# A chunked recurrence and a softplus feed-forward in one kernel: where the lowest three weight bits are made, another fixed order, and the written order kept six steps longer

## The chip, the cores and the metric

The kernel runs on one core of a Trainium2 chip. The metric is the device time of one execution in microseconds (us); lower is better. The kernel before takes 326.82 us, the median of three runs (325.9 to 327.14). One further execution was profiled. It took 326.83 us, of which the profile covers a span of 325.1 us from the first to the last instruction.

Engines are named as the profile does: PE (TensorE matmul), PEld (its weight loads), ACT (ScalarE), DVE (VectorE), POOL (GpSimd) and SP (SyncE, which issues all loads and stores here).

## What is computed

Inputs are `x` (4 x 8 x 768 x 32), decays `a` (4 x 8 x 768), `B` and `C` (4 x 8 x 768 x 16), and two weight matrices, `w_in` (256 x 2048) and `w_out` (2048 x 256).

```python
# per batch and head, in chunks of 32 tokens, with a carried state (16 x 32)
cum = np.cumsum(log(a), axis=-1)
M = (C @ B.T) * exp(cum_i - cum_j) * causal
y = M @ x + (C @ state) * exp(cum)
state = exp(sum(log a)) * state + sum_j B_j x_j exp(cum_last - cum_j)
# then, on all 3072 tokens with the 8 heads side by side (256 columns)
h = y @ w_in
g = softplus(h)
out = g @ w_out
```

The two weight matrices come as 64-bit floating-point numbers (a float32 draw times a 64-bit scalar). The chip receives a `low` and a `high` 32-bit word for each weight and makes a float32 number of them before it splits that into a high and a low part.

## The kernel before, in words

**Units.** Tokens are worked in 24 units of 128 (4 batches of 6). For unit `i` the recurrence makes scores (`S`, matmuls into `sp`), weighs them with decays (`D` on POOL makes `rm`, `M` on DVE makes `m`), updates the state (`U`, matmuls into `zp`, then DVE; `T` on DVE spreads it to `tb`), scales B and C (`B`, `C`: `bp`, `cc`), sums into `yp` (`R`, `I`), and splits the result into a high and a low part (`G`, `X`: `xh`, `xl`). The split into high and low parts lets a matmul product be made as three fast ones. From unit 8 on, `Q`, `cr`, `v` and `e` do the same for pairs of units.

**Feed-forward.** The 3072 tokens are six blocks `j` of 512, the 2048 hidden columns are 16 tiles `k` of 128. `F j.k` (function `first`) is six matmuls into `hp`, `P j.k` is three stages (softplus `e` on ACT, high part `gh` on ACT, low part `gl` on DVE), and `Z j.k` (function `second`) is six matmuls that add into the two accumulators `acc0`, `acc1`. `H k` is the first half of an `F0.k`. Blocks 0 and 1 are worked in two halves of eight `k` each, so their sums are put aside (`K`, `L`, and `keep_sums`) and added at the end (`finish`, whose `finish_part` adds `acc` and the kept `half` into `o` on DVE, line 803, and stores it).

**Weights.** There are 16 weight steps, eight for `w_in` (even) and eight for `w_out` (odd). `w n` loads 512 KB into a buffer `wraw` (four buffers, which are shared with the `bc` rows of units 8 and up). `W n` is five stages of the generator `split_stages`, one for each time that its name stands in the order:

1. ACT makes `w` (the high word times a power of two) and the sign, in the upper half-words of a buffer `signs` (two buffers, used in turn);
2. ACT makes the three lowest bits out of the `low` word and writes them in the lower half-words of `signs`;
3. DVE: `w = (w << 3) | signs`;
4. ACT: the high part (`wih` or `woh`);
5. DVE: the low part (`wil` or `wol`).

**Order.** Everything up to the end of the string `ORDER` is issued in the order of its words, and each engine works its own instructions of them strictly in that order. A word that stands several times runs the next stage each time. `warm n` is `n` matmuls of 512 columns on zeros, whose result is not used. After the string come steps `s` from `AHEAD` = 28 to 99 (96 feed-forward steps and a lag of four). At step `s` the loop issues `Z` of step `s - 4`, `F` and `P` of step `s`, and what `fills[s]` holds of the later units (12 and up): `split_whole` at `max(s0 - 4, 28)`, `attend_scores` at `s0`, `prefetch` of the unit three later at `s0 + 1`, with `s0` = 30, 34, 38, ... for unit 12, 13, 14, .... Up to `PINNED` = 31 (that is for s = 28, 29, 30) these too are kept as written. From there on a scheduler in the compiler arranges DVE, ACT and POOL instructions by its own estimate; matmuls and SP's transfers stay as written.

In the profile nearly every instruction of the kept order stands under line 129, the line of the helper that records it, so groups are told apart by their tiles. Later DVE, ACT and POOL instructions stand under their own lines: 290 and 292 (`split_unit`), 803 (`finish_part`), 720, 726, 732 (`P`'s three stages).

Of the kernel before, what the change touches and what calls it, by code (L numbers as in the profile page):

```python
# [45 lines left out]
THREE = 2.0**-29 * (1 - 2.0**-17)  # L46
DOWN = 5.7e-5 - 0.5
# [9 lines left out]


ORDER = """
la warm3 warm5 warm2 warm3 w2 w1 hc0 hc1 kb loga un0 un2 logr loga w0 logr gb growth hc2 ft0 W2 warm1 ft0 gq0 un1 W2  # L60
hc3 D0 gq2 growth W2 un3 W1 S0 w6 D1 gd fr2 M0 W1 fr0 hc4 fr2 gq2 fr0 W1 W2 fr0 S1 fr0 B2 hc5 W1 B0 M0 gq0 U0 un4 W1
D2 I0 M1 S2 W0 U0 G0 ft2 B1 T1 W0 M2 C1 W0 S3 B3 W0 M1 ft2 U1 W0 D3 R1 U1 C2 M2 U2 gg3 I1 U2 G0 T2 U3 fr2 D4 W6 G1 R2
U3 M3 I2 fr2 T3 W6 S4 X0 C3 T4 W6 S5 hc6 C4 G2 M3 w4 R3 G2 un6 B4 D5 M4 G1 R4 un5 tl I3 w3 M4 hc7 U4 X1 I4 D6 w5 M5 H0
un7 U4 G3 un8 W2 S6 G3 W6 X2 gg6 W4 X3 H1 G4 B6 W6 F0.0 C5 T5 H2 M5 W4 M6 F0.1 D9 W4 H3 P0.1 zero W3 F0.2 M6 R5 F0.3
P0.0 D7 P0.0 S7 W4 P0.2 U6 W4 I5 P0.1 U6 I6 P0.0 W3 un9 H4 M7 W5 w7 T7 Z0.0 W3 G4 G5 P0.2 B7 X4 F0.4 C7 M7 H5 P0.1 W5
D11 R7 G6 w10 F0.5 G6 gg8 Q8 X6 U7 P0.3 I7 P0.2 Q9 F0.6 G7 W5 W3 G7 W3 P0.3 Z0.1 Q9 P0.4 G5 X7 W7 F0.7 X5 Q8 P0.3 W7
Z0.2 C8 Q8 w8 cr9 P0.6 F1.0 P0.4 W5 P0.4 Z0.3 B8 P1.0 W5 Q9 W7 P1.0 F1.1 Q9 P0.5 B9 un10 P1.0 P0.5 Z0.4 U7 W8 T8 P0.5
F1.2 W7 Q8 P0.6 w12 P0.7 S9 gg12 F1.3 P0.7 cr8 P0.7 W7 Z0.5 P1.3 P0.6 P1.1 W8 F1.4 P1.2 W8 w14 P1.3 C9 Z0.6 W8 W8 F1.5
M9 P1.1 W10 M9 P1.1 Z0.7 D8 Q10 W10 F1.6 K0 L0 P1.3 P1.2 S8 W12 F1.7 M8 Q10 P1.4 Z1.0 M8 cr10 W10 D10 un11 B10 F0.8
W10 W12 P1.4 P1.2 w9 Z1.1 P1.5 W10 W12 W14 v8 Q10 P1.5 Z1.2 v8 P0.8 P1.5 W12 e8 W12 Z1.3 e8 e8 W9 Q10 gg10 F0.9 P1.4  # L70
P0.8 P1.6 P0.8 Q11 Z1.4 P1.7 Q11 P1.7 F0.10 W9 P1.7 W14 W9 S10 P1.6 Z1.5 M10 cr11 Q11 P1.6 w11 F0.11 W14 w15 Q11 w13
C10 Z1.6 P0.11 P0.9 W9 S11 W14 F0.12 P0.11 W14 C11 W11 M11 Z1.7 M11 P0.9 M10 F0.13 W11 K1 P0.10 W11 un13 v10 L1 W9 e8
P0.9 W15 Z0.8 v10 W11 e8 P0.10 e10 P0.12 P0.10 F0.14 e10 e10 e10 Z0.9 P0.14 e10 P0.12 W11 F0.15 P0.11 W13 P0.12 Z0.10
P0.14 W13 F1.8 W15 W13 un12 P0.15 P0.14 W13 Z0.11 W15 P0.15 W13 P0.13 F1.9 P0.15 P1.8 P0.13 P0.13 Z0.12 P1.9 F1.10
Z0.13 P1.10 W15 P1.9 W15 F1.11 P1.10 P1.9 P1.10 P1.8 Z0.14 P1.11 P1.8 P1.11 Z0.15 E0 P1.11
"""
# [30 lines left out]
def recurrence_then_ffn(ctx: ExitStack, tc: tile.TileContext, fst, un, alr, w_in, w_out, const, outT):  # L107
# [24 lines left out]
    V, A, Pl = (InOrder(e) for e in (nc.vector, nc.scalar, nc.gpsimd))  # L132
# [22 lines left out]
    gd = dr.tile([NB, NH, S], F32, name="gd")  # L155
# [689 lines left out]
    def both_scores(i):  # L847
# [152 lines left out]
```

## Time and profile before

| | |
|---|---|
| median of three runs | 326.82 us (325.9 to 327.14) |
| the profiled execution | 326.83 us |
| its span | 325.1 us |
| PE busy | 318.3 us (98%), 1974 matmuls |
| DVE busy | 190.6 us (59%), 338 instructions |
| ACT busy | 191.1 us (59%), 349 instructions |
| POOL busy | 39.4 us (12%), 42 instructions |
| DMA | 36.53 MB, a mean of 112 GB/s |

A row of a group has the line, the engine, the operation, the tiles written and read, the shape and the count, then the busy time, the mean of one in ns, and the idle time of the engine just ahead of them with what ended it. A row of the timeline has the start, the duration, the same names, and in brackets the idle time ahead of it. A table of stretches gives, for each, the busy time of the engines with instruction counts in brackets, the clock, the DMA share and GB/s. A matmul's end is modelled, so that two matmuls 227 ns apart are shown with 390 ns each; a PE that is shown as busy may still have small gaps.

### The profile page before, as it was taken

What the parts mean: (1) busy time and instruction counts of PE and PEld (TensorE: products, weight loads), DVE (VectorE), ACT (ScalarE), POOL (GpSimd) and SP (SyncE); (2) the same over time, 40 slices, a digit from 0 to 9 for tenths busy, and PEclk for the clock granted to TensorE, in tenths of its full rate; (3) what the DMA queues carried; (4) which work ended last, traced back from release to release, by engine and by line L of the source; (5) the groups of instructions that cost most, each with busy time, mean ns of one, the idle gap of its engine ahead of it and who ended that gap; (6) DMA issues with size and microseconds to landing.
All of it is one profiled execution on the core that took longest, in us unless ns stands there. A gap on an engine that the chain in (4) does not pass through costs nothing.

```text
span 325.1 us, 5266 instructions
## 1 busy us (share of the span) xinstructions
PE 318.3 (98%) x1974; PEld 255.7 (79%) x1974; DVE 190.6 (59%) x338; ACT 191.1 (59%) x349; POOL 39.4 (12%) x42
## 2 busy tenths in 40 slices
PE   8999999999999999899999999999999999999996
PEld 3568888888878888588888888888888888888885
DVE  3799767889584566775646746675744433322222
ACT  4898989797877565544433824644633344544450
POOL 3545300210300001102202101012100000000000
PEclk9999999999999999999999999999999999999999
DMA  6949658661732154335125246125201000100001
GB/s 222 394 152 359 212 187 214 176 194 46 246 100 66 65 151 124 107 124 143 32 99 159 70 130 146 51 97 161 86 14 34 0 2 0 53 12 2 1 0 65
DMA packets 25178, 36.53 MB, mean 112 GB/s; under 512 B 2112, under 2 KB 13504, under 8 KB 25152
## 3 DMA queue, kind: packets, MB, share of 16 engines
q1 hardware_dynamic: 25152, 36.19, 36.0%
q8 instruction: 15, 0.25, 0.3%
q14 instruction: 11, 0.09, 0.1%
HBM read 28.74 MB, written 3.24 MB: 98 GB/s over the span
## 4 chain that ended last, share of the span: by engine, by line
PE 88%; DVE 4%; DMA 3%; SPq 2%; issue 2%; ACT 0%; POOL 0%; DVEq 0%; ACTq 0%; POOLq 0%
PE hp L129 38%; PE acc L129 37%; PE yp L129 6%; PE sp L129 4%; PE warm L129 2%; DMA un<-in_un 2%; SPq L139 2%; DMA bc<-in_un 1%; PE zp L129 1%; PE end L129 1%; DVE m L129 1%; DVE w L129 1%; PE gp L129 0%; DVE b_rows L292 0%; DVE o L803 0%
## 5 line engine op out<-in xcount | busy, mean ns | idle before, releaser
L732 DVE TENSOR_TENSOR gl<-e,gh 128x512 fp32r<-128x512 f32 x65 | 49.8, 771 | 50.0 <-ACT gh L726 48.9
L129 PE MATMUL hp<-xh,wih 128*128 128x512 f32 (+1 forms) x204 | 77.6, 380 | 0.0
L129 PE MATMUL hp<-xl,wih 128*128 128x512 f32 (+1 forms) x204 | 76.9, 377 | 0.0
L129 PE MATMUL hp<-xh,wil 128*128 128x512 f32 (+1 forms) x204 | 76.8, 377 | 0.0
L720 ACT ACTIVATE e<-hp 128x512 f32<-128x512 f32 x65 | 38.7, 595 | 64.6 <-PE hp L129 64.2
L129 PE MATMUL acc<-gh,woh 128*128 128x512 f32 x188 | 74.9, 399 | 1.5 <-DVE o L803 1.5
L129 PE MATMUL acc<-gh,wol 128*128 128x512 f32 x188 | 73.4, 390 | 0.1
L129 PE MATMUL acc<-gl,woh 128*128 128x512 f32 x188 | 73.5, 391 | 0.0
L129 PEld LDWEIGHTS hp<-xh,wih 128*128 128x128 f32 x204 | 38.4, 188 | 8.3 <-DVE xl L129 1.0
L726 ACT CAST gh<-e 128x512 fp32r<-128x512 f32 x65 | 40.2, 619 | 6.7 <-PE acc L129 4.0
L129 PEld LDWEIGHTS hp<-xh,wil 128*128 128x128 f32 x204 | 38.3, 188 | 7.1
L129 PEld LDWEIGHTS hp<-xl,wih 128*128 128x128 f32 x204 | 38.4, 188 | 6.9
L129 PEld LDWEIGHTS acc<-gh,woh 128*128 128x128 f32 x188 | 35.4, 188 | 9.0 <-DVE o L803 1.4
L129 PEld LDWEIGHTS acc<-gh,wol 128*128 128x128 f32 x188 | 35.3, 188 | 8.1 <-DVE wol L129 0.6
L129 PEld LDWEIGHTS acc<-gl,woh 128*128 128x128 f32 x188 | 35.4, 188 | 6.4 <-DVE gl L732 0.2
L402 POOL TENSOR_SCALAR_AFFINE_SELECT rm<-fc 128x1024 f32<-128x1024 f32 x11 | 16.8, 1531 | 129.8 <-DVE m L457 97.2
L129 DVE TENSOR_TENSOR gl<-e,gh 128x512 fp32r<-128x512 f32 x31 | 21.5, 701 | 9.6 <-ACT gh L129 9.5
L129 POOL TENSOR_SCALAR_AFFINE_SELECT rm<-fc 128x1024 f32<-128x1024 f32 x13 | 19.0, 1466 | 63.5 <-DVE m L129 58.4
L129 ACT ACTIVATE signs<-wraw 128x512 f16<-128x512 f32 (+1 forms) x32 | 24.1, 776 | 0.0
L129 ACT ACTIVATE e<-hp 128x512 f32<-128x512 f32 x31 | 18.2, 594 | 7.5 <-PE hp L129 7.2
L129 ACT CAST gh<-e 128x512 fp32r<-128x512 f32 x31 | 19.0, 617 | 3.5 <-PE acc L129 3.3
L129 DVE TENSOR_TENSOR m<-sp,rm 128x512 f32<-128x512 f32 x26 | 17.2, 681 | 1.0 <-PE sp L129 1.0
(103 smaller groups left out, 306.8 us busy)
## 6 DMA issues: line engine op xcount, KB each, us to landing
bc<-in_un SPq DMA_DIRECT2D x16, 512.0 KB
wraw<-in_w_in SPq DMA_DIRECT2D x8, 512.0 KB
wraw<-in_w_out SPq DMA_DIRECT2D x8, 512.0 KB
un<-in_un SPq DMA_DIRECT2D x16, 256.0 KB
out_t<-o SPq DMA_DIRECT2D x9, 256.0 KB
gg<-gd SPq DMA_DIRECT2D x16, 128.0 KB
c_rows<-c_all SPq DMA_DIRECT2D x16, 128.0 KB
c_rows<-kc SPq DMA_DIRECT2D x16, 128.0 KB
```

Source lines behind the costliest of these rows:

```text
L129: return lambda *a, **k: tc.keep_in_program_order(f(*a, **k))
L139: tc.keep_in_program_order(nc.sync.dma_start(out, in_))
L402: Pl.affine_select(out=rm.rearrange("p h c i -> p (h c) i"), in_=fc[:, u].rearrange("p h c -> p (h c)").unsqueeze(2).broadcast_to([P, NH * ...
L720: A.activation(e, h, AF.Softplus)
L726: A.copy(gh, e)
L732: V.tensor_tensor(gl, e, gh.bitcast(F32), op=ALU.subtract)
```

## The change

Four things change.

- For weight steps 8 to 15 ACT no longer makes the lowest bits. In place of stage 2 (ACT) there is a second DVE instruction after stage 3: `w = (low >> 29) | w`. The count of stages is five as before. The raw buffer is read one stage later. Steps 0 to 7 are as before.
- The lower half-words of each `signs` buffer hold old bits of a step below 8, so POOL zeroes them, once for each of the two buffers, when a step of 8 or more first takes it.
- `ORDER` is another one. It has the same words, except that `warm3 warm5 warm2 warm3 ... warm1` (14 matmuls) is one `warm9`.
- `PINNED` is 37 in place of 31.

```diff
 ORDER = """
-la warm3 warm5 warm2 warm3 w2 w1 hc0 hc1 kb loga un0 un2 logr loga w0 logr gb growth hc2 ft0 W2 warm1 ft0 gq0 un1 W2
-hc3 D0 gq2 growth W2 un3 W1 S0 w6 D1 gd fr2 M0 W1 fr0 hc4 fr2 gq2 fr0 W1 W2 fr0 S1 fr0 B2 hc5 W1 B0 M0 gq0 U0 un4 W1
-D2 I0 M1 S2 W0 U0 G0 ft2 B1 T1 W0 M2 C1 W0 S3 B3 W0 M1 ft2 U1 W0 D3 R1 U1 C2 M2 U2 gg3 I1 U2 G0 T2 U3 fr2 D4 W6 G1 R2
-U3 M3 I2 fr2 T3 W6 S4 X0 C3 T4 W6 S5 hc6 C4 G2 M3 w4 R3 G2 un6 B4 D5 M4 G1 R4 un5 tl I3 w3 M4 hc7 U4 X1 I4 D6 w5 M5 H0
...
+la warm9 w2 hc0 un0 kb w0 loga un2 un1 logr loga hc1 logr ft0 gb growth hc2 gq0 ft0 hc3 S0 W2 D0 B0 hc5 w4 fr0 gq0 D1
+fr0 U0 M0 W2 fr2 fr0 W0 W2 ft2 U0 fr2 W2 T1 B2 S1 fr0 B1 W0 W2 growth M0 S2 ft2 gd W0 D2 un3 U1 C1 M1 un4 I0 hc4 M1 W0
+R1 w1 G0 D3 U2 M2 G0 I1 C2 U1 S3 M2 W4 W0 D5 S5 G1 gg3 M3 G1 gq2 C3 U2 T2 fr2 B3 R2 T3 fr2 gq2 X0 R3 X1 tl U3 M3 I2 B4
+I3 D4 U3 M5 W4 U4 H0 hc6 U4 W1 G2 w6 zero S4 un6 G3 G2 G3 H1 X2 hc7 C4 X3 un5 W4 F0.0 w3 T4 W4 un9 H2 P0.0 W4 F0.1 W1
...
-PINNED = 31
+PINNED = 37
+LOW = 8
...
+        halfwords = sign.bitcast(I16).rearrange("p (f t) -> p f t", t=2)
+        if step < LOW:
+            marked.add(id(sign))
+        elif id(sign) in marked:
+            marked.remove(id(sign))
+            Pl.memset(halfwords[:, :, 0], 0)
         A.activation(wf, high.bitcast(F32), AF.Copy, scale=REBIAS)
...
-        A.activation(
-            sign.bitcast(I16).rearrange("p (f t) -> p f t", t=2)[:, :, 0],
-            low.bitcast(U32),
-            AF.Copy,
-            bias=DOWN,
-            scale=THREE,
-        )
-        yield
+        if step < LOW:
+            A.activation(
+                halfwords[:, :, 0],
+                low.bitcast(U32),
+                AF.Copy,
+                bias=DOWN,
+                scale=THREE,
+            )
+            yield
         V.scalar_tensor_tensor(w, w, 3, sign, op0=ALU.logical_shift_left, op1=ALU.bitwise_or)
         signs.append(sign)
         yield
+        if step >= LOW:
+            V.scalar_tensor_tensor(w, low, 29, w, op0=ALU.logical_shift_right, op1=ALU.bitwise_or)
+            yield
         r = wf.rearrange(cut[0], **cut[1])
```

More of the change, by code (lines that the diff above doesn't have):

```diff
@@ L59 @@
 ORDER = """
-la warm3 warm5 warm2 warm3 w2 w1 hc0 hc1 kb loga un0 un2 logr loga w0 logr gb growth hc2 ft0 W2 warm1 ft0 gq0 un1 W2
-hc3 D0 gq2 growth W2 un3 W1 S0 w6 D1 gd fr2 M0 W1 fr0 hc4 fr2 gq2 fr0 W1 W2 fr0 S1 fr0 B2 hc5 W1 B0 M0 gq0 U0 un4 W1
-D2 I0 M1 S2 W0 U0 G0 ft2 B1 T1 W0 M2 C1 W0 S3 B3 W0 M1 ft2 U1 W0 D3 R1 U1 C2 M2 U2 gg3 I1 U2 G0 T2 U3 fr2 D4 W6 G1 R2
-U3 M3 I2 fr2 T3 W6 S4 X0 C3 T4 W6 S5 hc6 C4 G2 M3 w4 R3 G2 un6 B4 D5 M4 G1 R4 un5 tl I3 w3 M4 hc7 U4 X1 I4 D6 w5 M5 H0
-un7 U4 G3 un8 W2 S6 G3 W6 X2 gg6 W4 X3 H1 G4 B6 W6 F0.0 C5 T5 H2 M5 W4 M6 F0.1 D9 W4 H3 P0.1 zero W3 F0.2 M6 R5 F0.3
@@ L65 @@
[L65 to L74, printed above, removed]
@@ L75 @@
-Z0.13 P1.10 W15 P1.9 W15 F1.11 P1.10 P1.9 P1.10 P1.8 Z0.14 P1.11 P1.8 P1.11 Z0.15 E0 P1.11
+la warm9 w2 hc0 un0 kb w0 loga un2 un1 logr loga hc1 logr ft0 gb growth hc2 gq0 ft0 hc3 S0 W2 D0 B0 hc5 w4 fr0 gq0 D1
+fr0 U0 M0 W2 fr2 fr0 W0 W2 ft2 U0 fr2 W2 T1 B2 S1 fr0 B1 W0 W2 growth M0 S2 ft2 gd W0 D2 un3 U1 C1 M1 un4 I0 hc4 M1 W0
+R1 w1 G0 D3 U2 M2 G0 I1 C2 U1 S3 M2 W4 W0 D5 S5 G1 gg3 M3 G1 gq2 C3 U2 T2 fr2 B3 R2 T3 fr2 gq2 X0 R3 X1 tl U3 M3 I2 B4
+I3 D4 U3 M5 W4 U4 H0 hc6 U4 W1 G2 w6 zero S4 un6 G3 G2 G3 H1 X2 hc7 C4 X3 un5 W4 F0.0 w3 T4 W4 un9 H2 P0.0 W4 F0.1 W1
@@ new lines @@
+M4 R4 W6 W1 F0.2 M4 H3 P0.2 T5 D6 M5 P0.1 I4 W1 S6 G4 un7 P0.1 D9 w5 P0.0 S7 gg6 M6 G4 C5 X4 H4 P0.0 W6 W1 F0.3 P0.2
+W6 H5 P0.3 P0.1 W6 F0.4 B6 w7 W3 M6 Z0.0 W6 D7 P0.3 F0.5 W3 U6 W5 W3 I6 Z0.1 U6 un8 P0.2 P0.5 M7 P0.4 G6 W3 R5 F0.6 Q9
+W3 P0.4 Q9 C7 Z0.2 T7 B7 P0.3 W5 M7 G6 R7 w10 P0.5 W5 I5 cr9 D8 Q9 U7 I7 W7 Z0.3 G7 X6 P0.4 W5 G5 W7 F0.7 W5 G7 w14 G5
+X7 W10 Z0.4 X5 Q9 W7 P0.7 w8 F1.0 W10 P0.7 Q8 W10 S9 W7 P0.5 un11 F1.1 W10 P0.7 P0.6 Q8 P0.6 Z0.5 W7 cr8 P1.0 P0.6 W8
+F1.2 W10 Q8 W8 Z0.6 W14 W8 M9 un10 P1.2 F1.3 B9 W14 P1.0 gg10 P1.1 P1.0 Z0.7 P1.2 Q8 P1.3 B8 w12 W8 M9 F1.4 gg8 P1.3
@@ new lines @@
+U7 D11 K0 P1.1 W8 S8 L0 F1.5 M8 M8 Z1.0 P1.1 D10 T8 P1.4 F1.6 Q10 Q11 W14 Z1.1 P1.4 C8 w9 P1.2 W12 P1.4 F1.7 Q11 P1.5
+P1.3 P1.5 Z1.2 P1.6 W14 F0.8 P1.6 P1.6 Z1.3 W12 P0.8 Q10 F0.9 W12 cr10 P0.8 P1.5 Q10 w11 P1.7 v8 Q10 Q11 P0.8 P0.9 C9
+F0.10 v8 Q11 Z1.4 e8 e8 W14 S10 P1.7 Z1.5 M10 cr11 W12 W9 W12 w15 F0.11 P1.7 P0.10 C10 B10 W11 M10 W9 Z1.6 W11 e8 S11
+F0.12 gg12 M11 W11 w13 Z1.7 M11 P0.12 P0.9 P0.12 F0.13 P0.9 W9 K1 W9 v10 C11 L1 un12 W9 P0.10 P0.12 e8 F0.14 v10 P0.11
+P0.10 W11 e10 W13 Z0.8 e10 e10 W11 e10 F0.15 P0.11 e10 P0.14 P0.13 Z0.9 W15 F1.8 P0.13 P0.13 Z0.10 e8 P0.11 W13 F1.9
@@ L76 @@
+W15 W13 Z0.11 P1.9 un13 P0.14 W13 F1.10 P1.9 W13 P0.15 W15 Z0.12 P1.9 P0.14 P1.8 F1.11 P0.15 P1.10 P0.15 W15 Z0.13
+P1.8 W15 P1.11 P1.10 Z0.14 P1.10 P1.8 P1.11 Z0.15 E0 P1.11
 """
@@ L621, in pair_ends @@
         mid.pop(i), mid.pop(i + 1)
-    raws = {}
+    raws, marked = {}, set()
     def load_w(step):
```

## The prediction

> **What bounds the kernel now.** First the page: engine totals, slices, and the shares of the chain that ended last.
>
> ```profile
> PE 318.3 (98%) x1974; PEld 255.7 (79%) x1974; DVE 190.6 (59%) x338; ACT 191.1 (59%) x349; POOL 39.4 (12%) x42
> ...
> PE 88%; DVE 4%; DMA 3%; SPq 2%; issue 2%; ACT 0%; POOL 0%; DVEq 0%; ACTq 0%; POOLq 0%
> ```
>
> PE is the bound, at 98% of the span and 88% of the chain. An engine that becomes faster or slower elsewhere counts only where PE then waits more or less. So I look for PE's lost time: 325.1 - 318.3 = 6.8 us of idle, plus matmuls whose result is not used. The table of stretches says where the idle is.
>
> ```profile
> 0.00:10.00 10.00, 8.85 (x35) 4.14 (x36) 3.01 (x7) 5.43 (x10) 3.25 (x18) 1.00 0.76 253
> 10.00:20.00 10.00, 9.26 (x106) 5.32 (x104) 9.63 (x23) 9.45 (x27) 5.65 (x5) 1.00 0.90 337
> 20.00:30.00 10.00, 9.84 (x106) 6.97 (x107) 10.00 (x25) 8.36 (x23) 4.05 (x4) 1.00 0.70 230
> ...
> 80.00:90.00 10.00, 10.00 (x84) 8.08 (x82) 6.59 (x14) 6.56 (x12) 2.52 (x2) 1.00 0.65 210
> 90.00:100.00 10.00, 9.77 (x44) 7.61 (x43) 7.37 (x15) 8.35 (x15) 0.00 (x0) 1.00 0.28 82
> 100.00:110.00 10.00, 10.00 (x46) 8.27 (x45) 4.86 (x8) 5.97 (x12) 0.00 (x0) 1.00 0.17 52
> 110.00:120.00 10.00, 10.00 (x47) 8.17 (x46) 5.37 (x11) 5.92 (x10) 0.00 (x0) 1.00 0.49 152
> ...
> 130.00:140.00 10.00, 8.53 (x80) 6.22 (x79) 7.97 (x15) 4.56 (x8) 1.28 (x1) 1.00 0.33 100
> ...
> 300.00:325.10 25.10, 22.09 (x109) 18.46 (x107) 6.39 (x10) 9.12 (x15) 0.00 (x0) 0.99 0.06 21
> ```
>
> The first number after the comma is PE's busy time. It loses 1.15 us in the first stretch, 0.74 and 0.16 in the next two, 0.23 at 90, 1.47 at 130, and 3.0 at the end, where the last sums are stored. Everywhere else it loses nothing. The end is untouched by the change, so there are two places where it can gain: the front, and the wait near 135 us. In the front DVE is as full as PE (9.63 and 10.00 of 10), which will matter.
>
> **The front: 14 idle-work matmuls become 9.** From the timeline of PE, ACT, DVE and POOL, and the chain (the two rows in the middle, without an engine's tile arrows):
>
> ```profile
> 0.98 6.24 PE L129 MATMUL warm<-some 128*32 128x512 bf16 x13 [0.98 <-POOL some L129]
> 7.15 1.35 PE L129 MATMUL fp<-both_logs,kc 128*128 128x96 f32 x10
> 8.44 0.39 PE L129 MATMUL warm<-some 128*32 128x512 bf16 x1
> 10.29 1.13 PE L129 MATMUL sp<-head_in_l 64*128 64x512 f32 x4
> 18.42 0.68 PE L129 MATMUL yp<-cc,tb 128*128 128x128 f32 x4
> 25.82 0.39 PE L129 MATMUL hp<-xh,wih 128*128 128x256 f32 x1
> ...
> 2.49 2.31 PE warm L129 x5
> 4.84 1.02 PE warm L129 x2
> ...
> 3.62 0.64 ACT L129 ACTIVATE both_logs<-both_logs 128x192 f32<-128x192 f32 x2 [1.54 <-DVE both_logs L129]
> 8.54 0.87 ACT L129 ACTIVATE fc<-fp 128x384 f32<-128x384 f32 x1 [1.65 <-PE fp L129]
> 1.74 2.37 POOL L129 TENSOR_SCALAR_AFFINE_SELECT kc<-level 32x32 f32<-32x32 f32 x8 [0.74 <-DVE kc L129]
> 9.48 2.96 POOL L129 TENSOR_SCALAR_AFFINE_SELECT rm<-fc 128x1024 f32<-128x1024 f32 x2 [5.01 <-ACT ft L129]
> 10.15 1.15 DVE L129 SCALAR_TENSOR_TENSOR w<-w,signs 128x512 int32<-128x512 int32 x1 [4.69 <-ACT signs L129]
> ```
>
> The first useful matmul, `fp`, starts at 7.15. Its inputs are there at 4.3 at the latest (both logarithms end at 3.62 + 0.64, `kc` at 1.74 + 2.37). It waits for nothing but the 13 `warm` matmuls ahead of it in PE's order. In the new order 9 stand there, in one group. Five take 2.31 and two 1.02, so one more is (2.31 - 1.02) / 3 = 0.43; nine take 2.31 + 4 x 0.43 = 4.03 and end at 5.0. A matmul's last 0.15 us overlaps the next start (13 end at 7.22, `fp` starts at 7.15), so I put `fp` at 4.9, which is 2.25 us earlier. The fourteenth `warm` (8.44 to the end of its issue, about 0.3) goes too. Freed on PE: **2.55 us**.
>
> How much of it is kept depends on DVE, which is full from 10.15 to 30. The first matmuls of the feed-forward (`H0`, at 25.82) need what DVE makes. I counted the words of both orders ahead of `H0`: 41 DVE instructions before, 35 after; four of them in each are the early clips and sums, so 37 and 31 remain. The mean of one is 9.63 / 23 = 0.42. Before, 10.15 + 37 x 0.42 = 25.7, which is where `H0` stands; the count works. After, DVE's run begins when the chain `fp`, `fc`, `rm` allows the first `m`: `fc` starts 8.54 - 7.15 = 1.39 after `fp`, so at 6.3; `rm` starts 0.94 after `fc` and takes 1.48, so it ends at 8.7. Then 8.7 + 31 x 0.42 = 21.7 for `H0`. That is 4.1 us earlier. But three pieces of PE work have moved from ahead of `H0` to behind it (`S4`, `R4`, `I4`: an `sp` x4 at 1.13, a `yp` x4 at 0.68, and 16 small `yp` at about 0.4), 2.1 us together. What is kept is 4.1 - 2.1 = **2.0 us**. The bounds: 2.9 if DVE runs shorter than its mean and every wait ahead of `fp` goes as well; a loss of 0.6 if PE waits for loads instead. Loads are why it could be less; their sizes, in the list of transfers up to 30 us:
>
> ```profile
> wraw<-in_w_in SPq DMA_DIRECT2D x4, 512.0 KB
> ...
> head_in_l<-in_fst SPq DMA_DIRECT2D x4, 320.0 KB
> ...
> head_in_h<-in_fst SPq DMA_DIRECT2D x4, 256.0 KB
> ```
>
> SP's order changes from two weight loads first to one, and `hc1`, needed by the second unit, moves from the fifth load to the ninth, behind 2.73 MB in place of 1.86 MB (sums of these, with 0.3 MB for `la` and `kb`). At 253 GB/s 2.53 MB have come by 10 us, so it lands near 11, about when PE wants it.
>
> By the Trainium skill, page "TensorE: Matmul & The Clock Gate", Part 1, the array runs at half rate until some 3.4 us of sustained work. The trace shows half rate for longer, 0.43 for a `warm` against 0.23 for 512 columns later, in all of the first 13 from 0.98 to 7.15. By the page nine would be enough to warm it; by the trace this is open, and it is a rival below.
>
> **The wait at 135 us: written order to s = 36.** PE's waits, then the timeline around them:
>
> ```profile
> PE acc L129 <- DVE o L803: 1.5, 2, 0.9
> ...
> 127.22 0.45 SPq L139 DMA_DIRECT2D bc<-in_un  x1
> 131.52 0.72 ACT L290 ACTIVATE c_all<-bc,kb 128x512 fp32r<-128x512 f32 x1 [3.11 <-DMA bc<-in_un]
> 132.28 0.75 DVE L292 SCALAR_TENSOR_TENSOR c_all<-bc,kb,c_all 128x512 fp32r<-128x512 f32 x1 [1.86 <-ACT c_all L290]
> 132.94 1.28 DVE L457 TENSOR_TENSOR m<-sp,rm 128x512 f32<-128x512 f32 x2
> 134.14 0.68 DVE L803 TENSOR_TENSOR o<-acc,half 128x512 f32<-128x512 f32 x1
> 134.74 1.43 DVE L292 SCALAR_TENSOR_TENSOR b_rows<-bc,kb,b_rows 128x512 fp32r<-128x512 f32 x1
> 136.09 0.68 DVE L803 TENSOR_TENSOR o<-acc,half 128x512 f32<-128x512 f32 x1
> ...
> 107.43 2.72 PE acc L129 x12
> ```
>
> At s = 35 block 1 ends; its two accumulators must be emptied into `o` before block 2 starts in them at s = 36. The compiler's scheduler had moved a later unit's split (`c_all`, line 290) ahead. ACT sat 3.11 us for its load, DVE sat behind ACT, and `o`, whose sum was ready at 131.5, came at 134.14 and 136.09. PE lost 1.5 us.
>
> With `PINNED` 37, steps 31 to 36 keep the written order. At s = 34 DVE then has `gl`, two `m`, `bp`, `cc` and a split (two instructions), and at s = 35 the two `o`. Count from the end of s = 34's `hp`, with 1.36 per six matmuls (2.72 / 12): PE does `sp` (0.5), `acc` of s = 35, `hp`, `hp`, and wants the first accumulator at 0.5 + 3 x 1.36 = 4.6. DVE's `gl` comes after `e` and `gh`, at about 1.5, and behind it are 0.64 (`gl`), 1.28 (two `m`), 0.4 and 1.4 (split), then `o` 0.68: it ends at 5.9. So PE would still wait about 1.3, then find the second `o` done. What is kept is **0.4 us** less 0.2 for a turn of the pipeline that comes with each wait, say 0.3. Bounds: 1.5 gained if ACT and DVE are ahead of this count, 1.0 lost if one of the unit's loads comes late, since DVE's `o` and PE's `acc` then stand in line behind it with nothing allowed past.
>
> **Bits on DVE instead of ACT: nothing.**
>
> ```profile
> L129 ACT ACTIVATE signs<-wraw 128x512 int16<-128x512 uint32 x16 | 12.1, 773 | 0.0
> L129 DVE SCALAR_TENSOR_TENSOR w<-w,signs x16: 675/685/1150, 10.1 to 99.9; 128x512 int32<-128x512 int32 x16
> L129 POOL MEMSET c_rows<- 128x1024 f32 x1 | 1.0, 957 | 0.0
> ```
>
> ACT loses eight of 773 ns (6.2 us), DVE gains eight. The nearest row for `(low >> 29) | w` is the other shift-and-or of the same size, 685 ns, so 5.5 us; the upper bound is its slowest, 1150 ns, so 9.2. The lower is the same row's 675, since a second input is read either way. Between 80 and 120 DVE is busy 6.59 + 7.37 + 4.86 + 5.37 = 24.2 of 40 us, and with 9.2 more it is 33.4; PE is busy 39.8 there and covers it. Were that cover gone, it would cost 5.5 us. The two POOL memsets have half as many elements as the 957 ns row: 0.5 us each, or up to 1.0 if the stride of two halves the rate. POOL is idle from 90 to 120, so nothing waits for long. The raw buffer is held one DVE stage longer, about 0.7 us of a wait that begins far earlier.
>
> The 1150 ns stand in the row at 10.15, beside POOL's `rm` at 9.48. The Trainium skill, page "GPSIMD Engine Reference", section 1, says that POOL shares its SBUF interfaces with DVE when the latter reads two inputs; the trace agrees. By it a new instruction is slow only beside `rm`; the sum stays as it is.
>
> The rest of the order (0.23 idle at 90, and the new placing of everything to 108) I take at 0, with 0.5 either way: ACT and DVE are ahead of PE there.
>
> **Sum.** 2.0 + 0.3 + 0 = 2.3 us. The profiled execution's 326.83 equals the median, 326.82. So 326.8 - 2.3 = **324.5 us**.
>
> **Rivals.**
>
> 1. *Both gains are full.* DVE is quicker in the front (2.9) and the wait at 135 goes (1.5): 326.8 - 4.4 = 322.4. For it: PE idles only there. Against it: DVE is full in the front, and the count gives 1.3 us of wait at s = 36.
> 2. *PE waits for loads or DVE instead of doing idle work.* The 2.55 us of `warm` become idle time; only 0.3 or less remains: 326.5. For it: DMA is 0.76 to 0.90 busy in the first 20 us and DVE full from 10 to 30. Against it: `fp` starts a chain that DVE waited 4.69 us for.
> 3. *Slower: half rate in the front.* With nine `warm`, PE's clock could be released a few us later. It decides from the point where the half rate outlasts the `warm` group by more than about 3.5 us, that is beyond 8.5. Ahead of `H0` PE has some 14 us of useful work; if two thirds of this runs at half rate, it takes 9 us more, of which about 3 are covered by DVE's own run. 324.5 + 6 = 330. For it: the first full-rate `warm` is the one at 8.44 (0.39 against 1.02 for two). Against it: PE has `fp` and all behind it without a break, so it stays busy.
> 4. *Slower by a little: a late load at s = 31 to 36* with nothing allowed past it: the 1.0 lost there, and the front as in 2: 327.5.
>
> **How the numbers follow.** The forecast has 0.50, with its own range 323.3 to 325.4; rival 1 has 0.16, rival 2 0.21, rival 3 0.06, rival 4 0.07. Holding eight in ten from the lower part of rival 1 to rival 4: 322.6 to 327.5. A difference of 0.5% (1.6 us) is about what a measurement of this kernel can tell from no change; faster means below 325.2, slower above 328.4. Faster: 0.16 and nearly all of 0.50, 0.64. Same: rivals 2 and 4 and the rest of the forecast, 0.29. Slower: 0.07.
>
> **What would show it.** `fp` near 4.9 and the first `hp` near 21.7: the front is right; `fp` early and `hp` past 23: rival 2. Matmuls of 0.43 spacing after 8.5: rival 3. The waits of PE for `o` between 1.0 and 1.5: the count at s = 36 is right; none: rival 1; a wait for a load there: rival 4. DVE's rows with `low` at 0.69 and PE without idle from 80 to 120: the third part is right. The forecast is wrong if PE shows idle of more than 1 us between 30 and 110, which I put at nothing.

## The result: 1.2% slower, and the profile after

The changed kernel takes 330.44 us, the median of four executions (329.43 to 331.24), against 326.4 us (325.9 to 327.14) for the kernel before on the same chip. The ratio is 1.012, with a 95% interval of 1.0084 to 1.0157. The forecast was 324.5, in a range of 322.6 to 327.5. The profiled execution took 330.53 us, with a span of 328.8. In one run below (e11) one of the twelve executions took 331.61 us, at a mean granted clock of 0.979 and thus apart from the others, and is left out of the ratio.

The engine totals and the shares of the chain that ended last, from the page of the changed kernel:

```profile
PE 317.6 (97%) x1969; PEld 256.9 (78%) x1969; DVE 198.9 (61%) x348; ACT 185.5 (56%) x341; POOL 40.7 (12%) x44
...
PE 85%; DVE 5%; DMA 4%; ACT 3%; issue 2%; SPq 1%; POOL 0%; DVEq 0%; ACTq 0%; POOLq 0%
```

PE still sets the end. It is not busier (317.6 us, 318.3 before); it waits longer. The table of stretches of the changed kernel (after the comma PE's busy time, then the other engines, the granted clock, the DMA share and GB/s):

```profile
0.00:10.00 10.00, 8.83 (x48) 5.00 (x49) 4.97 (x11) 6.03 (x12) 5.32 (x19) 1.00 0.81 262
10.00:20.00 10.00, 8.96 (x91) 5.67 (x90) 10.00 (x25) 9.64 (x28) 4.60 (x4) 1.00 0.94 324
20.00:30.00 10.00, 8.48 (x98) 7.10 (x98) 6.73 (x16) 7.30 (x16) 2.24 (x3) 1.00 0.71 224
...
90.00:100.00 10.00, 9.43 (x44) 7.54 (x43) 6.91 (x14) 6.94 (x13) 0.00 (x0) 1.00 0.33 119
...
130.00:140.00 10.00, 6.19 (x27) 4.82 (x26) 9.10 (x17) 5.64 (x10) 1.41 (x1) 0.93 0.16 41
140.00:150.00 10.00, 10.00 (x87) 8.00 (x86) 6.15 (x16) 4.11 (x8) 0.00 (x0) 0.90 0.39 134
```

Before, PE lost 0.16 us from 20 to 30 and 1.47 from 130 to 140. Now it loses 1.52 and 3.81 there. The clock column (the last but two) is new as well: 0.93 and 0.90 where it was 1.00. This column counts half clock only from the first release on: in the first 5 us it says 1.00, although nine `warm` of 512 columns take 4.02 us there.

Three marks on PE's timeline tell how much of the difference arises where: the last `hp` matmul ahead of block 2's sums (the same work is done by then in both kernels), the first matmul into these sums, and the first of the group `end`. First the kernel before, then the changed one (in the row of the group, after the durations, stand the first and the last start):

```profile
134.03 0.39 PE L129 MATMUL hp<-xh,wil 128*128 128x512 f32 x1
134.97 0.47 PE L129 MATMUL acc<-gh,woh 128*128 128x512 f32 x1 [0.55 <-DVE o L803]
136.82 0.50 PE L129 MATMUL acc<-gh,woh 128*128 128x512 f32 x1 [0.92 <-DVE o L803]
L129 PE MATMUL end<-gh,woh x8: 281/283/283, 319.1 to 321.6; 128*128 128x256 f32 x8
```

```profile
134.10 0.39 PE L130 MATMUL hp<-xh,wil 128*128 128x512 f32 x1
138.30 0.47 PE L130 MATMUL acc<-gh,woh 128*128 128x512 f32 x1 [3.81 <-DVE o L130]
139.83 0.63 PE L130 MATMUL acc<-gl,woh 128*128 128x512 f32 x1
L130 PE MATMUL end<-gh,woh x8: 280/283/283, 322.7 to 325.2; 128*128 128x256 f32 x8
```

At 134 us the two kernels stand level (134.10 against 134.03): in this execution nothing is left of the gain in the front. From there on the changed kernel loses 322.7 - 319.1 = 3.6 us, and with 0.1 at 134 that is the difference of the spans, 328.8 - 325.1 = 3.7. Of the 3.6, the wait itself explains 2.1: 138.30 - 134.10 = 4.20, against 2.11 before (136.82 - 134.03, less three matmuls of 0.227 done in between). The other 1.5 lie behind the wait. In the changed kernel `acc` matmuls follow each other there at 0.43 us (a shown duration of 0.63) in place of 0.227. Its table of stretches, cut at the changes of the granted clock:

```profile
135.25:138.66 3.41, 0.36 (x2) 0.35 (x3) 3.41 (x7) 0.45 (x1) 0.44 (x1) 1.00 0.11 25
138.66:142.07 3.41, 3.41 (x38) 2.43 (x40) 2.09 (x6) 0.62 (x1) 0.00 (x0) 0.50 0.66 206
142.07:145.50 3.43, 3.43 (x37) 2.73 (x28) 1.72 (x6) 0.00 (x0) 0.00 (x0) 1.00 0.61 207
```

After 3.41 us in which PE was busy for 0.36, it runs at half clock for the next 3.41.

**Why the wait is 3.8 us.** (PE's wait for `o` is called the hole from here on.) Timeline of ACT and DVE in the changed kernel:

```profile
127.22 0.60 ACT L130 ACTIVATE e<-hp 128x512 f32<-128x512 f32 x1 [1.47 <-PE hp L130]
129.84 0.72 ACT L291 ACTIVATE c_all<-bc,kb 128x512 fp32r<-128x512 f32 x1 [2.02 <-DMA bc<-in_un]
130.47 0.60 ACT L130 CAST gh<-e 128x512 fp32r<-128x512 f32 x1
130.60 0.75 DVE L293 SCALAR_TENSOR_TENSOR c_all<-bc,kb,c_all 128x512 fp32r<-128x512 f32 x1 [4.12 <-ACT c_all L291]
...
132.87 1.28 DVE L130 TENSOR_TENSOR m<-sp,rm 128x512 f32<-128x512 f32 x2
...
134.47 1.35 DVE L418 TENSOR_TENSOR bp<-un,ft 128x128 f32<-128x128 f32 x1
...
136.15 0.74 DVE L130 SCALAR_TENSOR_TENSOR kc<-bc,kb,kc 128x512 fp32r<-128x512 f32 x1
136.81 0.74 DVE L130 SCALAR_TENSOR_TENSOR b_rows<-bc,kb,b_rows 128x512 fp32r<-128x512 f32 x1
137.47 1.27 DVE L130 TENSOR_TENSOR o<-acc,half 128x512 f32<-128x512 f32 x2
```

Rows under line 130 are in the kept order; rows under lines 291, 293 and 418 belong to steps from 37 on, which the scheduler may place freely. It put the split of unit 15 (planned at s = 38) on ACT ahead of the `gh` of s = 33. That split waits 2.02 us for its load, and DVE waits 4.12 behind it. Before, the same had happened, but the two `o` were free too, and the scheduler put them ahead of most of the rest: they came 1.9 and 3.8 us after the split's first DVE instruction (132.28, 134.14 and 136.09). It had also put the split of unit 14 (`kc`, `b_rows`, planned at s = 34) far ahead. DVE's timeline of the kernel before:

```profile
124.44 0.74 DVE L292 SCALAR_TENSOR_TENSOR kc<-bc,kb,kc 128x512 fp32r<-128x512 f32 x1
125.10 0.74 DVE L292 SCALAR_TENSOR_TENSOR b_rows<-bc,kb,b_rows 128x512 fp32r<-128x512 f32 x1
```

Now this split stands in its written place, right ahead of `o` (136.15 and 136.81), everything up to s = 36 stands in line behind the late split of unit 15, and `o` comes 6.9 us after it (137.47 - 130.60).

**The front.** PE's timeline, then DVE's and SP's rows and two pieces of the chain that bear on the one long wait:

```profile
0.98 4.02 PE L130 MATMUL warm<-some 128*32 128x512 bf16 x9 [0.98 <-POOL some L130]
4.93 1.63 PE L130 MATMUL fp<-both_logs,kc 128*128 128x96 f32 x10
21.52 0.39 PE L130 MATMUL hp<-xh,wih 128*128 128x256 f32 x1
25.62 0.39 PE L130 MATMUL hp<-xh,wih 128*128 128x256 f32 x1 [1.15 <-ACT xh L130]
...
24.70 0.42 DVE L130 TENSOR_TENSOR y<-yp,gg 128x256 f32<-128x256 f32 x1 [2.31 <-DMA gg<-gd]
...
14.37 0.43 SPq L140 DMA_DIRECT2D wraw<-in_w_out  x1
15.70 7.23 SPq L140 DMA_DIRECT2D gg<-gd  x8
...
14.37 8.23 DMA wraw<-in_w_out
22.62 2.00 DMA gg<-gd
```

`fp` is at 4.93 and the first `hp` at 21.52, 4.3 us earlier than before. But `gg3`, eight transfers that DVE needs for `y`, now stands behind `w1` on SP; its issue takes 7.23 us where it took 3.85, and PE waits 1.15 us in the first `F0.0` of this execution.

### The profile page after: what moved, and what is told of

Same layout as the page of the kernel before. It is cut to its first block, busy times and chain, and to the rows that moved or that the text cites. A ratio compares the mean times of both kernels' runs of the same rounds, so it can differ in the third digit from the quotient of the medians.

```text
span 328.8 us, 5261 instructions
## 1 busy us (share of the span) xinstructions
PE 317.6 (97%) x1969; PEld 256.9 (78%) x1969; DVE 198.9 (61%) x348; ACT 185.5 (56%) x341; POOL 40.7 (12%) x44
## 4 chain that ended last, share of the span: by engine, by line
PE 85%; DVE 5%; DMA 4%; ACT 3%; issue 2%; SPq 1%; POOL 0%; DVEq 0%; ACTq 0%; POOLq 0%
PE acc L130 37%; PE hp L130 36%; PE yp L130 5%; PE sp L130 3%; DMA wraw<-in_w_out 3%; DMA bc<-in_un 1%; PE warm L130 1%; DVE m L130 1%; PE zp L130 1%; PE end L130 1%; DVE w L130 1%; ACT signs L130 1%; DMA gg<-gd 1%; DVE gl L130 1%; ACT gh L130 1%
## 5 line engine op out<-in xcount | busy, mean ns | idle before, releaser
L130 DVE TENSOR_TENSOR m<-sp,rm 128x512 f32<-128x512 f32 x28 | 18.8, 682 | 1.9 <-PE sp L130 1.6
L130 ACT ACTIVATE signs<-wraw 128x512 f16<-128x512 f32 (+1 forms) x24 | 18.8, 784 | 0.0
```

The source lines that it names most:

```text
L130: return lambda *a, **k: tc.keep_in_program_order(f(*a, **k))
```

## The experiments

The experiments ran in four groups, each on another chip (e1 to e4, e5 to e8, e9 and e10, e11 and e12). The kernel before ran beside each group, with medians of 326.22, 326.13, 326.33 and 326.73 us; ratios are against it, and kernels of different groups are best compared by them. A ratio can differ by some 0.001 from that of the medians. With each execution comes its mean granted clock. One stretch of 3.41 us at half clock in a span of 325 is 0.5 x 3.41 / 325 = 0.005, so 0.996 or less means at least one. It does not say where the stretch lies; that is seen only in the one profiled execution of each kernel. The kernel before had none in 104 executions.

| kernel | order | warm | PINNED | bits of steps 8-15 | median us | ratio, 95% interval | at 0.996 or less |
|---|---|---|---|---|---|---|---|
| before | old | 14 | 31 | ACT | 326.4 | 1 | 0 of 104 |
| changed | new | 9 | 37 | DVE | 330.44 | 1.012, 1.0084 to 1.0157 | 4 of 4 |
| e2 | old | 14 | 37 | ACT | 331.02 | 1.0151, 1.0123 to 1.0179 | 6 of 6 |
| e4 | old | 14 | 31 | DVE | 327.79 | 1.0044, 1.0027 to 1.0061 | 0 of 12 |
| e12 | old | 9 | 31 | ACT | 325.2 | 0.9964, 0.9942 to 0.9985 | 3 of 12 |
| e5 | new | 9 | 31 | ACT | 325.18 | 0.9966, 0.9947 to 0.9984 | 5 of 9 |
| e1 | new | 9 | 31 | DVE | 324.95 | 0.9954, 0.9934 to 0.9975 | 4 of 12 |
| e6 | new | 14 | 31 | DVE | 325.88 | 0.9992, 0.9973 to 1.0012 | 1 of 12 |

The other runs (e3, e7 to e11) vary these and stand below.

**e1: the changed kernel with the old `PINNED`.**

```diff
-PINNED = 37
+PINNED = 31
```

> The changed kernel with PINNED back at 31. Theory: the loss is made at s = 35 and 36 alone. There the written order put DVE's two `o` behind two `m`, the split of unit 14 and what unit 15's early split had delayed; PE stood still for 4.2 us and then ran 3.4 us at half rate. With 31 the `o` may pass the split again, so PE's wait there should be 1 to 2 us as before, no half rate after it, and the time about 0.3 below the kernel before (326.1, between 325.6 and 326.8), since the front and the middle gained only 0.3. Rival: the other order string or the bits on DVE cost the time later too; then the time stays at 328.5 or more.

Measured: 324.95 us (323.52 to 326.35, 12 executions), ratio 0.9954. The profiled execution shows 0.66 us of wait for `o` and no half clock behind it. The whole loss is `PINNED`; the rest of the change gains 0.46%. That is more than expected: the median lies below the 325.6 to 326.8 of the theory.

**e2: the kernel before with the new `PINNED`.**

```diff
-PINNED = 31
+PINNED = 37
```

> The kernel before with PINNED 37 alone, its order and its bits unchanged. Theory: PINNED alone makes the loss, so PE waits 3.5 to 4.5 us for `o`, half rate follows, and the time is 329 to 331. Rival: the loss needs the new order string (other loads, other instructions on DVE); then the wait is below 2 us and the time 325.5 to 326.8.

Measured: 331.02 us, ratio 1.0151. PE waits 4.3 us for `o` in its profile, and every execution has a half-clock stretch. `PINNED` makes the loss in the old order as well, so neither the new order nor the bits are needed for it.

**e3: two steps more kept.**

```diff
-PINNED = 37
+PINNED = 39
```

> The changed kernel with PINNED 39, so that the split of unit 15 (s = 38), which the scheduler had put into ACT's line ahead of `gh` of s = 33, is kept in its written place as well. Theory: two things made the hole of 4.2 us, the intruding split (ACT waited 2.0 us for its load, DVE 4.1 us behind ACT) and the written order itself. Without the first the hole falls to about 1.3 to 1.6 us, as the prediction counted, the half rate goes, and the time is 326.3 to 327.3. Rival: the written order alone makes the hole; then it stays above 3 us and the time at 329.5 or more.

Measured: 327.96 us (326.44 to 329.79), ratio 1.0062 (1.0041 to 1.0084), 9 of 12 at 0.996 or less. The split of unit 15 is now kept too and comes behind `o`. Timeline of PE, DVE and POOL of this kernel:

```profile
136.12 0.47 PE L130 MATMUL acc<-gh,woh 128*128 128x512 f32 x1 [2.11 <-DVE o L130]
...
130.75 0.69 DVE L130 TENSOR_TENSOR gl<-e,gh 128x512 fp32r<-128x512 f32 x1 [2.03 <-ACT gh L130]
132.96 1.75 DVE L130 SCALAR_TENSOR_TENSOR kc<-bc,kb,kc 128x512 fp32r<-128x512 f32 x1
134.63 0.74 DVE L130 SCALAR_TENSOR_TENSOR b_rows<-bc,kb,b_rows 128x512 fp32r<-128x512 f32 x1
135.30 1.27 DVE L130 TENSOR_TENSOR o<-acc,half 128x512 f32<-128x512 f32 x2
...
132.77 1.42 POOL L403 TENSOR_SCALAR_AFFINE_SELECT rm<-fc 128x1024 f32<-128x1024 f32 x1 [10.26 <-DVE m L130]
```

This is the order that the prediction had counted, with nothing else in it: the wait is 2.11 us in place of the counted 1.3. The split of unit 14 takes 2.4 us (132.96 to the start of `o` at 135.30) where 1.4 was put: its first instruction runs beside POOL's `rm` and takes 1.75 in place of 0.74. So the written order by itself costs PE more than the scheduler's order did (1.47), and the work that the scheduler pulled ahead adds 1.7 us to that (3.81 - 2.11). The median lies beyond the theory's 326.3 to 327.3. The half-clock executions average 328.5 and the three others 326.81. The profiled one is among the three, so where the half clock of the nine lies is not shown.

**e11: the split of unit 15 alone kept behind.** `PINNED` stays 37.

```diff
         for f, args in fills[s]:
+            kept = in_order[0]
+            in_order[0] = kept or f == split_whole and args == (15,)
             f(*args)
+            in_order[0] = kept
```

> The changed kernel (PINNED 37) in which only the split of unit 15, planned at s = 38, keeps its written place behind the pinned steps, so that the scheduler cannot put it ahead of s = 33; PE's and SP's orders stay as they are. Theory (that split, waiting for its load with everything kept in order behind it, is what makes TensorE's hole longer than the written order counts): the hole before acc is 1.3 to 2.2 us, under 3.4, so no half-clock stretch behind it; 326.3 to 328.0 us. Rival (the written order alone makes it: gl, m, bp, cc and the split of unit 14 stand ahead of o): a hole of 3 us or more, 329 us or more.

Measured: 328.65 us (326.02 to 329.92, and 331.61 for the one left out), ratio 1.0065 (1.0042 to 1.0088). The hole is 2.78 us, between theory and rival: longer than in e3, since a free `bp` of 1.35 us still stands ahead of `o`. Of the 1.7 us of pulled-ahead work the split of unit 15 is thus 1.0 (3.81 - 2.78), and the free `bp` and `cc` are the other 0.7. The theory said no half clock under 3.4 us, and the profiled execution refutes that: half clock follows the hole. Of the eleven executions compared ten have a half-clock stretch, and the one without took 326.02, the least of them. Stretches of its profiled execution, cut at the clock's changes:

```profile
129.70:133.05 3.35, 3.35 (x16) 2.75 (x15) 2.77 (x6) 2.59 (x5) 0.75 (x1) 1.00 0.00 0
133.05:136.45 3.40, 0.62 (x4) 0.23 (x3) 3.40 (x7) 1.01 (x2) 0.66 (x1) 1.00 0.05 11
136.45:139.86 3.41, 3.41 (x30) 2.36 (x34) 1.22 (x5) 0.62 (x1) 0.00 (x0) 0.50 0.71 220
```

The hole (133.54 to 136.32) fell almost wholly into one stretch of 3.41 us and left PE 0.62 busy in it. In e3's profile the hole of 2.11 us left 1.78 of 3.41 busy in the emptier of its two stretches, and the clock stayed full:

```profile
132.23:135.64 3.41, 1.78 (x8) 1.13 (x6) 3.41 (x6) 1.82 (x3) 1.42 (x1) 1.00 0.00 0
```

The Trainium skill, page "TensorE: Matmul & The Clock Gate", Part 1, says that the clock is decided in windows of 3413 ns that run freely, not from the kernel's start. The trace agrees: the half-clock stretches shown here are all 3.41 us long, and the full-clock stretch ahead of the changed kernel's hole, from 5.54 to 138.66 us, is 133.12 us, 39 times 3.413. The first release came between 4.00 us (e9) and 6.97 us (the kernel before), though the first matmul started at 0.98 in both. The Trainium skill's rule of thumb in the same part of that page is that no idle gap longer than about 3.4 us should occur. Here 2.78 us was enough, and the measurement decides.

**e8: the hole filled with work.** `PINNED` stays 37. The twelve matmuls are extra and their result is used nowhere.

```diff
             begin(s)
+            if s == PINNED - 1:
+                hole = ps.tile([P, 512], F32, tag="ps", name="hole")
+                for _ in range(12):
+                    PE.matmul(hole, wih[:, 0, :P], x_parts(starts[2])[0][0][:, 0], start=True, stop=True)
         values(s)
```

> The changed kernel as it is (PINNED 37) with twelve 128x512 matmuls into an unused tile in TensorE's hole at 134 to 138 us, 12 times 0.227 us = 2.7 us of it; nothing else changes, and what VectorE and ScalarE do in the hole stays as it is. The twelve matmuls are extra work and their result is used nowhere. Theory (the hole is waiting for o, and a hole of over 3.4 us costs 1.7 us beside itself because TensorE runs at half clock for the next 3.4 us): acc starts at 138.3 as before, no half-clock stretch, 328.4 to 329.1 us. Rival (the half clock costs nothing beside the hole, because VectorE is late there anyway): 330.0 to 330.8 us.

Measured: 327.85 us (326.67 to 329.91), ratio 1.0054 (1.0035 to 1.0073). Waits and marks on PE's timeline of this kernel:

```profile
138.13 0.50 PE L130 MATMUL acc<-gh,woh 128*128 128x512 f32 x1 [1.40 <-DVE o L130]
138.47 0.39 PE L130 MATMUL acc<-gl,woh 128*128 128x512 f32 x1
...
L130 PE MATMUL end<-gh,woh x8: 280/283/283, 321.1 to 323.6; 128*128 128x256 f32 x8
```

`acc` starts as late as in the changed kernel (138.13 and 138.30), but at full rate, and `end` follows 183.0 us later instead of 184.4. So the half clock by itself costs 1.4 us in this comparison of profiles. The one half-clock stretch of this execution lies in the front, at 11.18 to 14.59 us, and none behind the hole. The time lies below the theory's 328.4 to 329.1: the medians differ by 2.6 us (2.2 by the ratios), more than the theory's 1.3 to 2.0. Two of the changed kernel's four executions had a mean clock of 0.99, that is two half-clock stretches, but this doesn't settle the rest.

**e4: the bits on DVE in the old order.**

```diff
-ORDER = """ (the new order)
+ORDER = """ (the order of before)
...
-PINNED = 37
+PINNED = 31
```

> The kernel before with the bits of steps 8 to 15 on DVE and the two POOL memsets, its order string and PINNED 31 unchanged. Theory: this part costs and gains nothing, PE has no idle between 100 and 120 and at most 0.6 us at 90, the time is within 0.5 us of the kernel before. Rival: DVE, with 5.5 us more work, is late for PE in the middle; then PE shows more than 1 us of idle between 80 and 110 and the time is 327.4 or more.

Measured: 327.79 us (326.5 to 328.73), ratio 1.0044: some 1.5 us slower, which is the rival's time. The rival's idle time of more than 1 us between 80 and 110 is not seen: the profile has 0.72 us. But the profiled execution was the quickest of the twelve, no slower than the kernel before, so only part of the loss can be seen. PE's timeline of e4:

```profile
91.33 0.50 PE L130 MATMUL acc<-gh,wol 128*128 128x512 f32 x1 [0.64 <-DVE wol L130]
```

Here it starts 1.03 us after the matmul ahead of it (at 90.30); before, it was 0.55 (90.46 and 89.91). The new DVE instruction (0.68 us) stands right ahead of the `wol` that this product needs. So about 0.5 us is put down to the bits; where the other 1.0 goes stays open.

**e5: the new order with all bits on ACT**, which is the order alone.

```diff
-PINNED = 37
-LOW = 8
+PINNED = 31
+LOW = 16
```

> The changed kernel's fixed order alone: PINNED back at 31 and LOW at 16, so that ScalarE makes the lowest bits of all sixteen weight steps as in the kernel before. Theory (the order is what gains, the bits on VectorE cost something in any order, as they cost 1.4 us in the old one): 324.0 to 325.0 us, as fast as the order with the bits on VectorE (324.95) or faster. Rival (the new order is laid out for the bits on VectorE; eight ACTIVATE of 0.69 us more on ScalarE make it late between 60 and 110 us): 325.7 to 327.0 us.

Measured: 325.18 us (323.61 to 326.44), against e1's 324.95. In the new order it makes no measurable difference which engine makes these bits. The 0.58 us that PE waits for `tb` at 91 us in e1 is gone, and a wait of 0.59 us ahead of other scores (`sp`, for ACT) at 61 us is there instead. The front of its profiled execution, cut at the clock's changes:

```profile
8.02:11.44 3.42, 2.40 (x28) 2.04 (x26) 3.16 (x10) 3.42 (x9) 1.66 (x2) 1.00 1.05 404
11.44:14.85 3.41, 3.41 (x8) 1.25 (x8) 2.90 (x5) 2.82 (x9) 1.61 (x1) 0.50 1.05 394
```

PE was 2.40 of 3.42 us busy, with narrow matmuls for the most part, and still the clock fell to half.

**e6: fourteen warm matmuls in the new order.**

```diff
-la warm9 w2 hc0
+la warm14 w2 hc0
...
-PINNED = 37
+PINNED = 31
```

> The changed kernel with PINNED 31 and fourteen warm matmuls instead of nine, in one run at the same place. Theory (in the new order the front is set by the loads and by VectorE, the five dropped warms only turned into idle time of TensorE): 324.9 to 325.6 us, first hp matmul at most 0.8 us later than 22.2. Rival (TensorE's own work sets the front, as the prediction counted: five times 0.43 us are paid in full): 326.6 to 327.2 us, first hp matmul some 2 us later.

Measured: 325.88 us (324.76 to 328.19), 0.93 above e1 (1.2 by the ratios), which lies between theory and rival: of the 2.1 us that five matmuls take, about half is paid. The first `hp` too lies between the two, at 23.24 against e1's 22.20. The ratio to before is 0.9992 (0.9973 to 1.0012). With the old number of warm matmuls, the new order and the bits on DVE together gain nothing that can be measured. But the same bits cost some 1.5 us in the old order (e4, 1.0044): the new order takes them without that loss.

**e12: nine warm matmuls in the old order.**

```diff
-la warm3 warm5 warm2 warm3 w2 w1 hc0
+la warm3 warm5 w2 w1 hc0
```

> The kernel before (old order, PINNED 31, all bits on ScalarE) with nine warm matmuls instead of fourteen: warm2 and warm3 are left out of the first group, the single one later stays. Theory (a shorter warm group lets the front fall back to half clock in some executions, whatever the order, and what TensorE saves turns into waits for VectorE): 3 or more of 12 executions with a mean granted clock of 0.996 or less, 325.6 to 326.5 us. Rival (the half-clock stretch comes with the new order, not with fewer warm matmuls; the five are worth 1 us or more as they were in the new order, where fourteen took 0.93 us more): at most one execution at 0.996 or less, 324.5 to 325.4 us.

Measured: 325.2 us (324.46 to 326.7), ratio 0.9964 (0.9942 to 0.9985), 3 of 12 with a half-clock stretch. On the clock the theory holds: half-clock stretches come with fewer warm matmuls in either order. That they lie in the front is seen in the profiles of e5 and e8, not in that of e12, which has none. On the time the rival does: the five are worth 1.5 us by the medians, 1.2 by the ratio. This one edit gains as much as the new order with its nine.

**e7: `gg3` ahead of `w1`.** `PINNED` 31; the first stage of weight step 1 moves behind `F0.0`.

```diff
-R1 w1 G0 ... G1 gg3 M3 ... U4 W1 G2 ... W4 F0.0 w3
+R1 gg3 w1 G0 ... G1 M3 ... U4 G2 ... W4 F0.0 W1 w3
```

> The changed kernel with PINNED 31, the load of gg3 ahead of the load of w1 on SyncE's queue, and the first stage of weight step 1 behind the first F product. Theory (gg3 behind w1 is what makes the F product wait, by up to 1.15 us, in some executions and less in others): 324.0 to 324.7 us. Rival 1 (that wait is taken up before 110 us anyway): 324.8 to 325.2 us. Rival 2 (w1 becomes late instead and ScalarE or TensorE waits for it later): 325.4 to 326.5 us.

Measured: 324.8 us (323.87 to 325.73), ratio 0.9958 (0.9941 to 0.9974), the lowest median of all, but by its ratio level with e1 (0.9954). The wait in `F0.0` is gone from the profile. It was gone from e1's profile too, and 0.42 in e3's, with the same order there. It varies, and is worth little in the median: rival 1.

**e9: e7 with three warm matmuls where PE waits for the second scores.**

```diff
-T1 B2 S1
+T1 B2 warm3 S1
```

> The kernel of e7 (PINNED 31, gg3 ahead of w1) with three more warm matmuls ahead of the second pair of scores (S1), where TensorE waited 0.2 to 1.2 us for head_in_l in the profiles. Theory (28 of 54 executions of the kernels with nine warm matmuls had a mean granted clock of 0.996 or less, none of 58 of the kernel before; it is a half-clock stretch of 3.4 us in the front, which three matmuls in that hole keep away): at most 2 of 12 executions at 0.996 or less, 324.0 to 324.7 us. Rival 1 (the stretch has nothing to do with that hole): 4 or more of 12, 324.6 to 325.6 us. Rival 2 (the three matmuls lie on the path, 0.3 us each): clock as in the theory, 325.2 to 326.0 us.

Measured: 325.15 us (324.32 to 326.11), ratio 0.9964 (0.9948 to 0.9979), and not one of 12 executions at 0.996 or less. PE's timeline and the stretch of its clock window:

```profile
10.23 0.82 PE L130 MATMUL warm<-some 128*32 128x512 bf16 x3
11.61 1.13 PE L130 MATMUL sp<-head_in_l 64*128 64x512 f32 x4 [0.56 <-DMA head_in_l<-in_fst]
...
7.41:10.82 3.41, 3.38 (x31) 2.19 (x27) 3.07 (x9) 3.34 (x7) 1.99 (x2) 1.00 1.04 393
```

On the clock the theory holds: the three keep the half clock away, and e10 below, with the same three, has none in 12 either. But the kernel is no faster for it: 325.15 misses the theory's 324.0 to 324.7 and is close to rival 2's 325.2 to 326.0. Whether the three lie on the path, as rival 2 has it, is not shown. What a half-clock stretch costs in the front is not settled: the executions with one average 324.93 against 324.6 in e7 and 325.15 against 325.02 in e5, in e12 even 325.15 against 325.48, but 1.0 us more than the others in e1 and 1.6 in e8, with 3 to 9 executions on each side.

**e10: e9 with all bits on ACT.**

```diff
-LOW = 8
+LOW = 16
```

> The kernel of e9 with LOW at 16, all lowest bits on ScalarE. Theory (in the new order it makes no difference which engine makes the bits of steps 8 to 15; 325.18 against 324.95 us so far): within 0.5 us of e9. Rival (VectorE is the later of the two from 80 to 110 us, where TensorE waits 0.58 us for tb with the bits on VectorE and not without them): 0.5 to 0.8 us below e9.

Measured: 325.52 us (324.46 to 326.34), 0.37 above e9: within 0.5, as the theory had it, and once more no clear difference between the engines.

## Why the prediction was wrong

The forecast was 326.8 - 2.3 = 324.5, and 330.44 came: 5.9 us more. In the profiled executions this splits into 2.1 + 2.4 + 1.5 = 6.0.

**The wait at s = 36: "0.4 us less 0.2 for a turn of the pipeline, say 0.3" gained, and 2.1 lost (2.4 of the miss).** This is the step that failed, with its lower bound of "1.0 lost". It failed in two ways. The count took the written order as all that DVE has to do. But steps from 37 on are still the scheduler's, and it sends them ahead of kept ones: the split of unit 15 and a `bp` came between, and DVE sat 4.12 us for a load. The prediction had read the row in which the scheduler pulled that split ahead, and took it as cured by `PINNED`; what `PINNED` took away was that `o` could pass it. It also moved the split of unit 14 from 124.44 us to the place right ahead of `o`. The bound did name a late load "with nothing allowed past it", and rival 4 was the mechanism, but at a price of 1.0 and a chance of 0.07, both too small. The second error is the size of the split of unit 14, 1.4 against 2.4 us; with it and nothing else the wait is the 2.11 of e3, already more than the 1.47 before. So no gain was to be had here from keeping the written order. The term's own figures give less than it says: 1.5 us before less the counted 1.3 is 0.2, not 0.4, and no row here shows the 0.2 for a turn of the pipeline.

**The half clock behind the hole (1.5 of the miss) was not in the sum at all.** Rival 3 looked for half rate in the front, for want of warm matmuls. It came at 138 us, behind 4 us without any matmul. A wait of 3.8 us cost 1.5 more by the clock behind it.

**The front: "2.0 us" kept, nothing left at 134 us in this execution (2.1 of the miss, with the 0.07 that it is behind there).** The steps up to the first `hp` are right: `fp` at 4.93 (4.9 was put), the first `hp` at 21.52 (21.7). (By its rows the overlap of two matmuls is 0.07, not 0.15, and the three moved pieces are 2.2 us, not 2.1; neither changes much.) But by the tables PE is idle for 3.73 us of the first 30 now, where it was 2.05. Of the 2.15 us of five `warm` (5 x 0.43) 1.68 became idle time, and another 0.34 went at 90 us (9.43 busy for 9.77). The bound named loads, and one was late: PE's 1.15 us for `gg3`. That is rival 2 (no gain in the front) in this execution. Over the medians the front fares better: e1 gains 1.3 us, the shorter wait at 135 us included, and e12 1.5 with the warm matmuls alone. So the term was mis-sized by 0.5 or more in the median. Its reason, DVE's count over the new order, is not borne out: with the bits on ACT and nine warm matmuls the new order (e5, 0.9966) and the old one (e12, 0.9964) are level.

**Rival 3, half rate in the front, happens, but not as put.** The clock is released at 5.54 us in the changed kernel (the trace's record of the granted clock), well before the 8.5 from which it was to decide. It falls back later, in some executions, for 3.41 us, and the executions that have it take from nothing to 1.6 us more (e12, e5, e7, e1, e8), not 6.

**Bits on DVE: "nothing" is right in the new order (e1 against e5, e9 against e10) and wrong by 1.5 us in the old one (e4).** The groups of DVE in the changed kernel (ns, minimum, median, maximum):

```profile
L130 DVE SCALAR_TENSOR_TENSOR w<-wraw,w x8: 676/684/1746, 50.8 to 102.6; 128x512 int32<-128x512 int32 x8
```

The price from the nearest row, 685 ns, is right at the median; the slowest took 1746, above the bound of 1150. POOL's two memsets took 694 ns each, within the 0.5 to 1.0 us put for them. The cover was named by shares of busy time over 40 us, and those do not say whether one product waits for one instruction.

**The test "wrong if PE shows idle of more than 1 us between 30 and 110"** was not met (0.57); what went wrong lay outside it.

## What to carry to other kernels

To keep a written order for longer gives a scheduler's freedom away on one side only: free work can still be put ahead of kept work, and kept work can no longer step past it. Where such a border is moved, read what the free side has waiting for loads, and whether the instruction that empties the accumulators stands behind it. Fill or split a hole of a few us on TensorE, since its price includes the clock behind it; and take warm-up matmuls away one group at a time, for here that single edit (e12) gained as much as a whole new order with the same nine (e5).

## What the runs showed of the hardware

- A hole of 2.78 us that lay almost wholly in one stretch of 3.41 us (0.62 busy) brought half clock for the next 3.41 us (e11). A hole of 2.11 us that left 1.78 busy did not (e3). The same kernel has a half-clock stretch in one execution and none in another (e11 is without one in 1 of 11, e3 in 3 of 12, though some of these stretches may lie in the front).
- TensorE that was shown busy for 2.40 of 3.42 us, with narrow matmuls for the most part, fell to half clock as well (e5). With three more matmuls of 512 columns the stretch was 3.38 busy and kept its clock (e9). So the busy time shown does not decide by itself: 2.40 lost the clock here, and 1.78 kept it in e3.
- Instructions of DVE beside POOL's `rm` took 1.35 us (`bp` in the changed kernel and e11, usually 0.28) and 1.75 us (`kc` in e3, otherwise 0.74).
